# Two accumulators share one output buffer on their way out of a fused attention and softplus-FFN kernel

## The chip, the cores and the metric

The kernel runs on one core of a Trainium2 chip. Its engines work in parallel and are tied by semaphores: TensorE (PE in the profile; its weight loads are listed as PEld), VectorE (DVE), ScalarE (ACT), GpSimd (POOL) and SyncE (SP), which here issues the DMAs. TensorE reads its operands from SBUF and writes to PSUM; results go from PSUM to SBUF by a copy on VectorE or ScalarE, and from SBUF to HBM by a DMA.

The metric is the device time of one execution in microseconds, the median of several runs. All times here are in microseconds (us) unless marked ns.

## What is computed

Eight batches of 576 tokens and 8 heads of width 64. A small set of 32 packed queries per head first attends to all keys and values; then every token attends to the 32 packed results, which serve as its keys and its values. The heads are joined to 512 columns, and a feed-forward layer with softplus follows.

```python
def sm_attn(qq, kk, vv):
    s = scale * np.matmul(qq, kk.transpose(0, 1, 3, 2))
    s = s - np.max(s, axis=-1, keepdims=True)
    a = np.exp(s)
    a = a / (np.sum(a, axis=-1, keepdims=True) + 1e-09)
    return np.matmul(a, vv)
p_packed = sm_attn(p, k, v)
out = sm_attn(q, p_packed, p_packed)
...
h = x @ w_in                     # x: 4608 x 512, w_in: 512 x 2048
g = np.maximum(h, 0.0) + np.log1p(np.exp(-np.abs(h)))
return (g @ w_out).astype(np.float32)      # w_out: 2048 x 512
```

## The kernel before

The hidden layer of 2048 columns is cut into `NF` = 16 blocks of 128. A **unit** is one block of one batch; the main loop (from line 718) runs over the 8 x 16 units in order, batch by batch. Batches are counted from 0.

For each unit, `gemm1` (line 595) makes the 576 hidden values of 128 columns in two halves of 288, in two PSUM buffers named `ph`: twelve matmuls, since each product is taken in three parts (high by high, high by low, low by high) to keep precision. `softplus` turns `ph` into `e`: absolute value, exponential and logarithm on ScalarE (lines 617, 619, 620), maximum and sum on VectorE (line 622), which is the last reader of `ph`. Then `split` (lines 609, 610) cuts the first 512 tokens of `e` into a high part `gh` and a low part `gl` on VectorE. The last 64 tokens go to a collecting tile `rest` on GpSimd (line 626).

Two units later (`LAG` = 2), `gemm2_tile` (line 633) multiplies `gh` and `gl` with the unit's rows of the output weights, three matmuls for each of the `NT` = 4 groups of 128 tokens, and adds them to four PSUM accumulators `acc`. The pool `ps_acc` holds four such buffers and no more. With the sixteenth unit of a batch, the accumulator of a group is complete and `store` (line 648) takes it out: a copy on VectorE (line 650) to an SBUF tile `o`, and from there a DMA or two on SyncE (line 654). Directly behind, the first unit of the next batch begins to add to the same four PSUM buffers, so its first matmul on each waits for that buffer's copy.

Behind an odd batch the 64 remaining tokens of that batch and of the one before it form a fifth group of 128. `rests` (line 657) splits them, 256 columns at a time, into `gh_m` and `gl_m`, runs 48 matmuls into one more buffer of `ps_acc` (`acc_m`), and stores that too. Behind an even batch nothing comes between.

The tiles `o` lie in the pool `cv` under the tag `x`, with two buffers. The same two buffers carry weights in 64-bit form early in the kernel (`load64`, 512 numbers of 8 bytes for each partition), so each is 4 KB long in each partition; an `o` of 512 numbers of 4 bytes fills half of one. The third copy of a batch so takes the buffer of the first, and the fourth that of the second, when the store from it has landed.

In between, the attention of the next batch is worked off in small steps that the main loop draws from a generator (`attention_next` for batches 2 and later). Its names with two numbers, such as `m_4_0`, are those of batch and head group: maximum `m` (line 280), `nm` (282), exponential (287), sum `rs` (292, 293), scores `ps` (267), packed values and the second softmax (lines 334 to 358).

TensorE's order is the one in which the program issues its instructions. The order on the other engines is laid out by a scheduler when the program is built, which follows its own estimate of when each operand and each buffer is there; on the chip each engine then works through its queue in that order.

Of the kernel before, what the change touches and what calls it, by code (L numbers as in the profile page):

```python
# [9 lines left out]
F32 = mybir.dt.float32  # L10
# [16 lines left out]
def pack_attention_then_softplus_ffn(  # L27
# [13 lines left out]
    DM, DFF = w_in.shape  # L41
    P = 128
# [7 lines left out]
    NT = S // P  # L50
    REST = S - NT * P
# [8 lines left out]
    cv = ctx.enter_context(tc.tile_pool(name="cv", bufs=1))  # L60
# [16 lines left out]
    def rest_at(b, f):  # L77

        return f + NF if f < LAG and b // 2 % 2 else f
# [15 lines left out]
    def load_pack(bg, queues):  # L95

        t = cv.tile([PW, H, D], F32, tag="m", name=f"p_{bg}", bufs=1)
        for i in range(BG):
            queues[i % len(queues)].dma_start(
                t[i * J:(i + 1) * J], p[bg * BG + i].rearrange("h j d -> j h d")  # L100
            )
        return t

    def pack_transposed(bg, t):
        for o in range(0, H, HG):
            ps = bank(f"ppt_{bg}_{o}")
            for i in range(HG):
                nc.tensor.transpose(
                    ps[:D, i * PW:(i + 1) * PW], t[:, o + i, :], ident[:PW, :PW]
                )  # L110
            dst = pT[:, o:o + HG, :].rearrange("x h j -> x (h j)")
            nc.vector.tensor_copy(dst[:D], ps[:D, :HG * PW])
            nc.scalar.copy(dst[D:], ps[:D, :HG * PW])
# [414 lines left out]
    def attention(b):  # L528
        return attention_first(b) if b < FIRST else attention_next(b)
# [16 lines left out]
    def m_cols(b):  # L546

        return MC if b else MC // 2
# [30 lines left out]
    def gemm1(b, f, res):  # L579

        n = m_cols(b)
        halves = res["m"][f * P // n]
        at_h, at_l = res["at"]
        phs = []
        for c in range(2):
            ph = ps_h.tile([P, 512], F32, tag="h", name=f"ph_{b}_{f}_{c}")
            phs.append(ph[:, :C])
            i = 0
            for g in range(G):
                mh, ml = halves[g * n // MC]  # L590
                o = g * n % MC + f * P % n
                ms = slice(o, o + P)
                cs = slice(c * C, (c + 1) * C)
                for x, y in ((mh, at_h), (mh, at_l), (ml, at_h)):
                    nc.tensor.matmul(  # L595
                        ph[:, :C], x[:, ms], y[:, g, cs],
                        start=(i == 0), stop=(i == 3 * G - 1),
                    )
                    i += 1
        return phs  # L600

    def halves(nm):
        return [
            work.tile([P, NT * P], F32R, tag=t, name=f"{t}_{nm}", bufs=LAG + 1)
            for t in ("gh", "gl")
        ]

    def split(hi, lo, x):
        nc.vector.tensor_copy(hi, x)  # L609
        nc.vector.tensor_tensor(lo, x, hi.bitcast(F32), op=ALU.subtract)  # L610

    def softplus(b, f, hv, done):
        e = work.tile([P, S], F32, tag="e", name=f"e_{b}_{f}")
        es = [e[:, c * C:(c + 1) * C] for c in range(2)]
        spans = [e] if b == 0 else es
        for c in range(2):
            nc.scalar.activation(es[c], hv[c], AF.Abs)  # L617
            for x in spans[c:c + 1] if b else spans[:c]:
                nc.scalar.activation(x, x, AF.Exp, scale=-1.0)  # L619
                nc.scalar.activation(x, x, AF.Ln, bias=1.0)  # L620
        for c in range(2):
            nc.vector.scalar_tensor_tensor(es[c], hv[c], 0.0, es[c], op0=ALU.max, op1=ALU.add)  # L622
        yield
        yield
        r = (b % 2) * REST
        nc.gpsimd.tensor_copy(rest[:, rest_at(b, f), r:r + REST], e[:, NT * P:])  # L626
        yield
        done[b, f] = halves(f"{b}_{f}")
        split(*done[b, f], e[:, :NT * P])

    def gemm2_tile(acc, gh, gl, f, cs, first, last):
        for i, (x, y) in enumerate(((gh, wo_h), (gh, wo_l), (gl, wo_h))):
            nc.tensor.matmul(  # L633
                acc, x[:, cs], y[:, f, :],
                start=(first and i == 0), stop=(last and i == 2),
            )

    def rows(b, col, n):
        o = out[b * S:(b + 1) * S, :]
        c, t = divmod(col, C)  # L640
        if b < FIRST:
            i, x = divmod(t, NP)
            n = min(n, NP - x)
            return n, o.rearrange("(x s) e -> s x e", s=SI)[2 * i + c, x:x + n, :]
        n = min(n, C - t)
        return n, o.rearrange("(t c) e -> c t e", c=2)[c, t:t + n, :]

    def store(acc, pieces, nm):
        o = cv.tile([P, DM], F32, tag="x", name=f"o_{nm}", bufs=2)
        nc.vector.tensor_copy(o, acc)  # L650
        for row, b, col, n in pieces:
            while n:
                m, dst = rows(b, col, n)
                nc.sync.dma_start(dst, o[row:row + m, :])
                row, col, n = row + m, col + m, n - m

    def rests(b):


        fs = sorted(range(NF), key=lambda x: rest_at(b, x))  # L660
        gh, gl = halves(f"{b}_m")
        n = NT // 2
        for i in range(0, NF, n):
            o = rest_at(b, fs[i])
            c = i % NT * P
            cs = slice(c, c + n * P)
            split(gh[:, cs], gl[:, cs], rest[:, o:o + n, :].rearrange("x f j -> x (f j)"))
            if i == 0:
                yield
                am = ps_acc.tile([P, DM], F32, tag="acc", name=f"acc_{b}_m")  # L670
            for t in range(n):
                gemm2_tile(
                    am, gh, gl, fs[i + t], slice(c + t * P, c + (t + 1) * P),
                    i + t == 0, i + t == NF - 1,
                )
        store(am, [(0, b - 1, NT * P, REST), (REST, b, NT * P, REST)], f"{b}_m")
        yield


# [35 lines left out]
    gs, acc = {}, None  # L715
    units = [(b, f) for b in range(B) for f in range(NF)]
    ahead, chain, due = iter(()), iter(()), 0.0
    for u in range(len(units) + LAG):
        if u < len(units):
            b, f = units[u]  # L720
            if f == 0:
                if (b + 1) % BG == 0 and b + 1 < B:
                    pack_transposed((b + 1) // BG, pt)
                ahead = attention(b + 1) if b + 1 < B else iter(())
                due = 0.0
            chain = softplus(b, f, gemm1(b, f, res[b]), gs)
            next(chain)
            if f == NF - 1:
                if (b + 2) % BG == 0 and b + 2 < B:
                    pt = load_pack((b + 2) // BG, (nc.sync,))  # L730
                for _ in ahead:
                    pass
                if b + 1 < B:
                    weights(b + 1)
        if u >= LAG:
            b2, f2 = units[u - LAG]
            gh, gl = gs.pop((b2, f2))
            if f2 == 0:
                acc = [ps_acc.tile([P, DM], F32, tag="acc", name=f"acc_{b2}_{t}") for t in range(NT)]
        last = u >= LAG and f2 == NF - 1 and b2 % 2 == 1  # L740
        if last:
            both = rests(b2)
            next(both)
        for t in range(NT):
            if u >= LAG:
                gemm2_tile(
                    acc[t], gh, gl, f2, slice(t * P, (t + 1) * P), f2 == 0, f2 == NF - 1
                )
                if f2 == NF - 1:
                    store(acc[t], [(0, b2, t * P, P)], f"{b2}_{t}")  # L750
            if u < len(units):
                due += PACE if b != FIRST - 1 else PACE_FIRST
                while due >= 1:
                    next(ahead, None)
                    due -= 1
                if b == 0:
                    cdue += CONV
                    while cdue >= 1:
                        next(conv, None)
                        cdue -= 1  # L760
            next(chain, None)
        if last:
            next(both)
        if u + 2 < len(units):


            nb, c = units[u + 2][0], units[u + 2][1] * P
            if c % m_cols(nb) == 0:
                make_m(nb, c // m_cols(nb), res[nb])
# [29 lines left out]
```

## Time and profile before

| what | value |
| --- | --- |
| runs, median (lowest to highest) | 786.67 us (784.75 to 788.64) |
| the profiled execution, as a whole | 781.94 us |
| its span in the trace | 780.2 us |
| granted TensorE clock, mean | 0.995 |
| copies of accumulators, line 650 | 32 from `acc`, median 683 ns, first start at 161.7 us, last at 767.0; 4 from `acc_m` of 691 to 692 ns |
| store of an `o`, issue to landing | 1.6 / 2.2 / 4.3 us (least, median, most) |
| share of all DMA engines' time, main queue | 31.4% |

The span is that of the instructions in the trace; the execution has 1.74 us around it. A row of the timeline gives start, duration, engine, line, operation, output and inputs, and in brackets how long the engine sat idle before it and what ended that wait. Buffer numbers are left out of the names, so all four accumulators are `acc` there. The copies of batches 0 to 7 start near 162, 248, 341, 424, 517, 600, 693 and 763 us.

### The profile page before, as it was taken

How to read it: one execution, taken by the hardware profiler on the slowest of the kernel's cores; microseconds unless marked ns; L12 is line 12 of the kernel's file. 1: busy time of each engine (PE TensorE's matmuls, PEld its weight loads, DVE VectorE, ACT ScalarE, POOL GpSimd, SP SyncE). 2: the span in 40 equal slices, each digit the busy share in tenths (PEclk: the TensorE clock that was granted, in tenths of full speed). 3: DMA queues.
4: the chain of work that ended last, by engine and by line, in shares of the span. 5: the costliest groups of instructions: out<-in, count | busy, mean ns of one | idle time of the engine just before them, and what ended most of it. 6: DMA issues, size and time to landing. Idle time of an engine off the chain costs nothing.

```text
span 780.2 us, 14340 instructions
## 1 busy us (share of the span) xinstructions
PE 737.2 (94%) x5360; PEld 580.6 (74%) x5360; DVE 536.8 (69%) x1220; ACT 437.0 (56%) x1089; POOL 93.9 (12%) x166
## 2 busy tenths in 40 slices
PE   6568998889999999999999999999999999999997
PEld 4346675767877787878787787878787787888886
DVE  3788879965778559675877559665887559574553
ACT  6658877655555355566456355565456355565540
POOL 1414433100000000000000000000000000000010
PEclk9999999999999999999999999999999999999999
DMA  9965755424411432025311423025311400010002
GB/s 240 258 159 153 192 137 146 85 60 73 81 32 35 95 54 70 1 70 83 62 31 38 91 47 77 2 56 90 62 32 34 95 2 2 1 55 1 1 1 68
DMA packets 149669, 55.97 MB, mean 72 GB/s; under 512 B 116320, under 2 KB 142944, under 8 KB 149600
## 3 DMA queue, kind: packets, MB, share of 16 engines
q1 hardware_dynamic: 149328, 55.00, 31.4%
q8 instruction: 42, 0.69, 0.4%
q14 instruction: 27, 0.22, 0.1%
q10 hardware_dynamic: 272, 0.07, 0.0%
HBM read 45.61 MB, written 9.44 MB: 71 GB/s over the span
## 4 chain that ended last, share of the span: by engine, by line
PE 81%; DVE 8%; ACT 5%; DMA 3%; issue 2%; POOL 1%; SPq 0%; DVEq 0%; ACTq 0%; POOLq 0%
PE acc L633 40%; PE ph L595 25%; PE acc_m L633 6%; PE psm L558 4%; PE ps L267 2%; PE psp L310 1%; DMA q<-in_q 1%; PE psa L300 1%; DMA x_i<-in_moe_w_in 1%; DVE t L203 1%; ACT e L619 1%; DVE e L622 1%; ACT e L620 1%; ACT m L192 1%; DVE wo_l L236 1%
## 5 line engine op out<-in xcount | busy, mean ns | idle before, releaser
L633 PE MATMUL acc<-wo_h,gh 128*128 128x512 f32 x512 | 208.5, 407 | 5.8 <-DVE o L650 5.8
L622 DVE SCALAR_TENSOR_TENSOR e<-ph,e 128x288 f32<-128x288 f32 x256 | 113.3, 451 | 137.9 <-ACT e L620 135.6
L617 ACT ACTIVATE e<-ph 128x288 f32<-128x288 f32 x256 | 102.7, 402 | 177.9 <-PE ph L595 135.8
L633 PE MATMUL acc<-wo_l,gh 128*128 128x512 f32 x512 | 201.6, 394 | 0.0
L633 PE MATMUL acc<-wo_h,gl 128*128 128x512 f32 x512 | 201.3, 393 | 0.0
L595 PE MATMUL ph<-at_h,mh 128*128 128x288 f32 x512 | 158.7, 310 | 6.9 <-DVE e L622 5.5
L595 PE MATMUL ph<-at_l,mh 128*128 128x288 f32 x512 | 153.0, 299 | 4.3 <-DVE at_l L541 4.3
L595 PE MATMUL ph<-at_h,ml 128*128 128x288 f32 x512 | 153.1, 299 | 0.0
L595 PEld LDWEIGHTS ph<-at_h,mh 128*128 128x128 f32 x512 | 97.4, 190 | 42.9 <-issue 13.9
L633 PEld LDWEIGHTS acc<-wo_h,gh 128*128 128x128 f32 x512 | 96.7, 189 | 32.4 <-DVE o L650 8.2
L626 POOL COPY rest<-e 128x64 f32<-128x64 f32 x128 | 48.3, 378 | 582.8 <-DVE e L622 551.4
L633 PEld LDWEIGHTS acc<-wo_h,gl 128*128 128x128 f32 x512 | 96.6, 189 | 21.5
L619 ACT ACTIVATE e<-e 128x288 f32<-128x288 f32 (+1 forms) x240 | 109.2, 455 | 3.9
L620 ACT ACTIVATE e<-e 128x288 f32<-128x288 f32 (+1 forms) x240 | 109.4, 456 | 3.1
L633 PEld LDWEIGHTS acc<-wo_l,gh 128*128 128x128 f32 x512 | 96.9, 189 | 13.0
L595 PEld LDWEIGHTS ph<-at_l,mh 128*128 128x128 f32 x512 | 97.8, 191 | 7.7 <-DVE at_l L541 5.0
L595 PEld LDWEIGHTS ph<-at_h,ml 128*128 128x128 f32 x512 | 97.8, 191 | 0.0
L610 DVE TENSOR_TENSOR gl<-e,gh 128x512 fp32r<-128x512 f32 x128 | 91.0, 711 | 7.0 <-DVE gh L609 1.4
L573 ACT CAST mh<-psm 128x512 fp32r<-128x512 f32 (+1 forms) x72 | 35.7, 540 | 62.4 <-PE psm L558 62.4
L609 DVE CAST gh<-e 128x512 fp32r<-128x512 f32 x128 | 55.5, 433 | 5.8
L574 DVE TENSOR_TENSOR ml<-psm,mh 128x512 fp32r<-128x512 f32 (+1 forms) x72 | 42.8, 622 | 21.3 <-ACT mh L573 20.7
L558 PE MATMUL psm<-w_in_sb,pt 64*32 64x512 f32 (+1 forms) x576 | 42.3, 567 | 3.4 <-ACT T_q L260 1.2
(75 smaller groups left out, 719.3 us busy)
## 6 DMA issues: line engine op xcount, KB each, us to landing
v<-in_v SPq DMA_DIRECT2D x16, 576.0 KB, 4.8
x_i<-in_moe_w_in SPq DMA_DIRECT2D x32, 256.0 KB, 4.2
x_o<-in_moe_w_out SPq DMA_DIRECT2D x16, 512.0 KB, 4.2
k<-in_k SPq DMA_DIRECT2D x48, 144.0 KB, 3.2
q<-in_q SPq DMA_DIRECT2D x48, 144.0 KB, 3.1
out<-o SPq DMA_DIRECT2D x18, 256.0 KB, 2.2
k<-in_k SPq DMA_DIRECT2D x4, 576.0 KB, 8.6
q<-in_q SPq DMA_DIRECT2D x4, 576.0 KB, 7.3
```

The costliest lines, as they stand in the source:

```text
L558: nc.tensor.matmul(ps[hh * J:(hh + 1) * J, :n], res["pt"][g][o:o + D, hh * J:(hh + 1) * J], w_in_sb[o:o + D, hh, c * n:(c + 1) * n], start ...
L573: nc.scalar.copy(mh[:, cols], ps[:, :n])
L574: nc.vector.tensor_tensor(ml[:, cols], ps[:, :n], mh[:, cols].bitcast(F32), op=ALU.subtract)
L595: nc.tensor.matmul(ph[:, :C], x[:, ms], y[:, g, cs], start=(i == 0), stop=(i == 3 * G - 1),)
L609: nc.vector.tensor_copy(hi, x)
L610: nc.vector.tensor_tensor(lo, x, hi.bitcast(F32), op=ALU.subtract)
L617: nc.scalar.activation(es[c], hv[c], AF.Abs)
L619: nc.scalar.activation(x, x, AF.Exp, scale=-1.0)
L620: nc.scalar.activation(x, x, AF.Ln, bias=1.0)
L622: nc.vector.scalar_tensor_tensor(es[c], hv[c], 0.0, es[c], op0=ALU.max, op1=ALU.add)
L626: nc.gpsimd.tensor_copy(rest[:, rest_at(b, f), r:r + REST], e[:, NT * P:])
L633: nc.tensor.matmul(acc, x[:, cs], y[:, f, :], start=(first and i == 0), stop=(last and i == 2),)
```

## The change

Two accumulators share one tile. For an even group `t` a tile of 128 x 2 x 512 numbers, which fills a whole 4 KB buffer, is taken from the same two buffers; the even group's copy fills its first half and the odd group's its second. So a batch's four copies take two tiles, one per buffer, and the copy of the rests (`t` = 4) takes a third for itself. The stores are the same rows as before, read from a half of the tile.

```diff
-    def store(acc, pieces, nm):
-        o = cv.tile([P, DM], F32, tag="x", name=f"o_{nm}", bufs=2)
+    half = []
+
+    def store(acc, pieces, nm, t):
+        if t % 2 == 0:
+            half[:] = [cv.tile([P, 2, DM], F32, tag="x", name=f"o_{nm}", bufs=2)]
+        o = half[0][:, t % 2, :]
         nc.vector.tensor_copy(o, acc)
...
-        store(am, [(0, b - 1, NT * P, REST), (REST, b, NT * P, REST)], f"{b}_m")
+        store(am, [(0, b - 1, NT * P, REST), (REST, b, NT * P, REST)], f"{b}_m", NT)
...
-                    store(acc[t], [(0, b2, t * P, P)], f"{b2}_{t}")
+                    store(acc[t], [(0, b2, t * P, P)], f"{b2}_{t}", t)
```

The order on TensorE and GpSimd does not change. On VectorE, the copies move, and with them some rows of the attention. In the rows below a name's first number is that of the accumulator or of the unit within its batch, and the last one counts buffers; the change makes `o_0` the tile of accumulators 0 and 1 and `o_2` that of 2 and 3, and line 650 becomes line 654.

VectorE behind batch 0, from the second copy on; before:

```order
L650 COPY o_1_1955<-acc_1_719 128x512
L609 CAST gh_1_1969<-e_1_1934 128x512
L610 TENSOR_TENSOR gl_1_1970<-e_1_1934,gh_1_1969 128x512
L622 SCALAR_TENSOR_TENSOR e_2_1994<-ph_2_0_1980,e_2_1994 128x288
L622 SCALAR_TENSOR_TENSOR e_2_1994<-ph_2_1_1987,e_2_1994 128x288
L650 COPY o_2_1963<-acc_2_720 128x512
L609 CAST gh_2_2019<-e_2_1994 128x512
L610 TENSOR_TENSOR gl_2_2020<-e_2_1994,gh_2_2019 128x512
L650 COPY o_3_1976<-acc_3_721 128x512
```

The same place with the change:

```order
L654 COPY o_0_1946<-acc_1_719 128x512
L654 COPY o_2_1962<-acc_2_720 128x512
L609 CAST gh_1_1968<-e_1_1934 128x512
L654 COPY o_2_1962<-acc_3_721 128x512
L610 TENSOR_TENSOR gl_1_1969<-e_1_1934,gh_1_1968 128x512
L622 SCALAR_TENSOR_TENSOR e_2_1992<-ph_2_0_1978,e_2_1992 128x288
L622 SCALAR_TENSOR_TENSOR e_2_1992<-ph_2_1_1985,e_2_1992 128x288
```

The third and fourth copies now stand around the split of unit 1, ahead of the softplus of unit 2, and no longer among and behind the work of unit 2.

VectorE behind batch 2, in the time of batch 3, from the split of unit 1 on; before:

```order
L609 CAST gh_1_4021<-e_1_3980 128x512
L280 TENSOR_REDUCE m_4_0_4031<-a_4_0_3951 128x1
L610 TENSOR_TENSOR gl_1_4022<-e_1_3980,gh_1_4021 128x512
L650 COPY o_2_4017<-acc_2_3072 128x512
L282 TENSOR_SCALAR nm_4_0_4033<-m_4_0_4031 128x1
L292 TENSOR_SCALAR rs_0_4144<-z_4_0_4072 128x1
L293 RECIPROCAL rs_0_4144<-rs_0_4144 128x1
L622 SCALAR_TENSOR_TENSOR e_2_4051<-ph_2_0_4037,e_2_4051 128x288
L622 SCALAR_TENSOR_TENSOR e_2_4051<-ph_2_1_4044,e_2_4051 128x288
L609 CAST gh_2_4093<-e_2_4051 128x512
L650 COPY o_3_4028<-acc_3_3073 128x512
L610 TENSOR_TENSOR gl_2_4094<-e_2_4051,gh_2_4093 128x512
```

With the change:

```order
L609 CAST gh_1_4016<-e_1_3976 128x512
L654 COPY o_2_4012<-acc_2_3068 128x512
L610 TENSOR_TENSOR gl_1_4017<-e_1_3976,gh_1_4016 128x512
L654 COPY o_2_4012<-acc_3_3069 128x512
L280 TENSOR_REDUCE m_4_0_4025<-a_4_0_3947 128x1
L282 TENSOR_SCALAR nm_4_0_4027<-m_4_0_4025 128x1
L622 SCALAR_TENSOR_TENSOR e_2_4045<-ph_2_0_4031,e_2_4045 128x288
L292 TENSOR_SCALAR rs_0_4138<-z_4_0_4066 128x1
L293 RECIPROCAL rs_0_4138<-rs_0_4138 128x1
L622 SCALAR_TENSOR_TENSOR e_2_4045<-ph_2_1_4038,e_2_4045 128x288
L609 CAST gh_2_4087<-e_2_4045 128x512
L610 TENSOR_TENSOR gl_2_4088<-e_2_4045,gh_2_4087 128x512
```

The fourth copy moves from behind the first half of unit 2's split to directly behind unit 1's, and the softmax maximum of the attention moves behind it. Behind batch 4 the rows are the same.

VectorE behind batch 1, with the splits of the rests, from the second copy on; before:

```order
L650 COPY o_1_2939<-acc_1_2004 128x512
L280 TENSOR_REDUCE m_3_0_2974<-a_3_0_2887 128x1
L609 CAST gh_1_2963<-e_1_2916 128x512
L282 TENSOR_SCALAR nm_3_0_2976<-m_3_0_2974 128x1
L610 TENSOR_TENSOR gl_1_2964<-e_1_2916,gh_1_2963 128x512
L650 COPY o_2_2959<-acc_2_2005 128x512
L609 CAST gh_m<-rest 128x256
L292 TENSOR_SCALAR rs_0_3154<-z_3_0_3082 128x1
L610 TENSOR_TENSOR gl_m<-rest,gh_m 128x256
L293 RECIPROCAL rs_0_3154<-rs_0_3154 128x1
L609 CAST gh_m<-rest 128x256
L650 COPY o_3_2970<-acc_3_2006 128x512
```

With the change:

```order
L654 COPY o_0_2930<-acc_1_2002 128x512
L280 TENSOR_REDUCE m_3_0_2970<-a_3_0_2885 128x1
L654 COPY o_2_2956<-acc_2_2003 128x512
L609 CAST gh_1_2960<-e_1_2914 128x512
L654 COPY o_2_2956<-acc_3_2004 128x512
L610 TENSOR_TENSOR gl_1_2961<-e_1_2914,gh_1_2960 128x512
L282 TENSOR_SCALAR nm_3_0_2972<-m_3_0_2970 128x1
L609 CAST gh_m<-rest 128x256
L610 TENSOR_TENSOR gl_m<-rest,gh_m 128x256
L609 CAST gh_m<-rest 128x256
L610 TENSOR_TENSOR gl_m<-rest,gh_m 128x256
L292 TENSOR_SCALAR rs_0_3150<-z_3_0_3078 128x1
```

The first split of the rests in these rows now has three copies in the rows ahead of it, where it had two, and `nm` stands six places behind the second copy in place of three. Behind batch 4 and batch 2, in the time of batches 3 and 5, rows of the second softmax also change places with rows of units 7 and 8, on VectorE and ScalarE. On SyncE the stores of a batch follow each other more closely, and query loads that stood between them come behind.

## The prediction

> **What bounds the kernel now.** I read the page first, for the busy shares and the costliest groups, then the waits of TensorE, then the timelines of TensorE and VectorE around the places that the waits point to.
>
> ```profile
> span 780.2 us, 14340 instructions
> PE 737.2 (94%) x5360; PEld 580.6 (74%) x5360; DVE 536.8 (69%) x1220; ACT 437.0 (56%) x1089; POOL 93.9 (12%) x166
> L633 PE MATMUL acc<-wo_h,gh 128*128 128x512 f32 x512 | 208.5, 407 | 5.8 <-DVE o L650 5.8
> ```
>
> TensorE (PE) is busy 94% of the span, VectorE (DVE) 69%. The costliest group, the first of the three matmuls that add a unit to an accumulator, has 5.8 us of idle time ahead of it, all ended by the copy in line 650, which is one of the lines that change. When does TensorE wait at all? The first of the changed copies starts at 161.7 us (table ahead of this prediction), and up to it the order of instructions is the same on every engine, so only the time behind it counts. These are all waits of TensorE from 130 us on (microseconds in total, times, longest), and its busy time from 161 us to 780 us:
>
> ```profile
> PE acc L633 <- DVE o L650: 5.8, 4, 1.9
> PE ph L595 <- DVE e L622: 2.0, 1, 2.0
> PE psm L558 <- DVE a L334: 0.6, 1, 0.6
> PE psm L558 <- POOL w_in_sb L211: 0.5, 1, 0.5
> PE ps L267 <- ACT T_q L260: 0.2, 1, 0.2
> 161.00:780.00 619.00, 608.15 (x4360) 486.32 (x4358) 414.27 (x946) 322.89 (x843) 42.51 (x111) 1.00 0.23 47
> ```
>
> In the window TensorE is busy (first figure behind the window's length) 608.15 of 619 us at a granted clock of 1.00; VectorE has 414.27, ScalarE 322.89. The span ends with the copy of the last accumulator and its store:
>
> ```profile
> 775.61 0.69 DVE L650 COPY o_m<-acc_m 128x512 f32<-128x512 f32 x1 [2.12 <-PE acc_m L633]
> ```
>
> So the last matmul sets the end, and time that leaves TensorE's queue there leaves the span, as long as VectorE and ScalarE, which serve it, keep up.
>
> **What the waits cost.** Batches count from 0. Behind an even batch (0, 2, 4, 6) the next batch's first unit needs the four accumulators at once; behind an odd one the rests come between. The first such place lies in the time of batch 1:
>
> ```profile
> 166.26 0.40 PE L633 MATMUL acc<-wo_h,gl 128*128 128x512 f32 x1
> 168.03 0.49 PE L633 MATMUL acc<-wo_h,gh 128*128 128x512 f32 x1 [1.37 <-DVE o L650]
> 168.36 0.39 PE L633 MATMUL acc<-wo_l,gh 128*128 128x512 f32 x1
> 168.59 0.40 PE L633 MATMUL acc<-wo_h,gl 128*128 128x512 f32 x1
> 170.11 0.50 PE L633 MATMUL acc<-wo_h,gh 128*128 128x512 f32 x1 [1.12 <-DVE o L650]
> 170.45 0.40 PE L633 MATMUL acc<-wo_l,gh 128*128 128x512 f32 x1
> ```
>
> Ends of matmuls are modelled and overlap, so I go by starts. Undisturbed, one starts 0.23 us after the other (168.36 to 168.59). Here 166.26 to 168.03 is 1.77, too long by 1.54, and the next step of 0.33 is too long by 0.10. The second wait costs 1.52 - 0.23 = 1.29 and 0.34 - 0.23 = 0.11. Together **3.04 us**. The other three, in the time of batches 3, 5 and 7, with an undisturbed passage from the score matmuls to an accumulator as a measure (its two rows come first):
>
> ```profile
> 248.84 0.72 PE L267 MATMUL ps<-k,pT 64*32 64x288 f32 x16
> 249.48 0.50 PE L633 MATMUL acc<-wo_h,gh 128*128 128x512 f32 x1
> ...
> 347.69 0.72 PE L267 MATMUL ps<-k,pT 64*32 64x288 f32 x16
> 349.89 0.50 PE L633 MATMUL acc<-wo_h,gh 128*128 128x512 f32 x1 [1.48 <-DVE o L650]
> ...
> 523.58 0.71 PE L267 MATMUL ps<-k,pT 64*32 64x288 f32 x16
> 526.16 0.50 PE L633 MATMUL acc<-wo_h,gh 128*128 128x512 f32 x1 [1.87 <-DVE o L650]
> ...
> 697.87 0.39 PE L633 MATMUL acc<-wo_h,gl 128*128 128x512 f32 x1
> 698.22 0.50 PE L633 MATMUL acc<-wo_h,gh 128*128 128x512 f32 x1
> 698.55 0.40 PE L633 MATMUL acc<-wo_l,gh 128*128 128x512 f32 x1
> ```
>
> Undisturbed the passage takes 0.64. In batch 3 it takes 2.20, so **1.56** are lost; in batch 5 2.58, so **1.94**; in batch 7 the steps of 0.35 and 0.33 are too long by 0.12 and 0.10, **0.22**. The four places cost 3.04 + 1.56 + 1.94 + 0.22 = **6.76 us**.
>
> **Why the copies come late.** VectorE works its queue in order. In batch 3:
>
> ```profile
> 344.76 0.68 DVE L650 COPY o<-acc 128x512 f32<-128x512 f32 x1
> ...
> 346.67 0.15 DVE L292 TENSOR_SCALAR rs<-z 128x1 f32<-128x1 f32 x1 [1.17 <-ACT a L287]
> ...
> 348.25 0.46 DVE L622 SCALAR_TENSOR_TENSOR e<-ph,e 128x288 f32<-128x288 f32 x1 [0.72 <-ACT e L620]
> ...
> 349.15 0.68 DVE L650 COPY o<-acc 128x512 f32<-128x512 f32 x1
> ```
>
> The third copy starts at 344.76, the fourth not before 349.15, and TensorE goes on at 349.89. By these rows no accumulator or store holds that copy at 349.15: it stands behind the next unit's work in the queue, which itself waits for ScalarE (1.17 and 0.72). The queue was laid out with the third and fourth copies behind the landing of the first two stores, whose buffers they took. With the change they need no such buffer, and in the order of the changed kernel the third stands directly ahead of the split of the next unit or just behind its first half, and the fourth at most two rows on, behind all eight batches.
>
> **The change, part by part.** The copies and stores stay the same in number and size (36 copies of about 0.68 us); nothing is added or removed on TensorE, whose order is the same row for row. Each second-half copy waits in the order for TensorE alone, not for the store of the first half.
>
> Removed: the 6.76 us. In batch 3 the fourth copy can now start about 344.7 and end at 345.4, three microseconds ahead of its use at 348.33 (347.69 + 0.64); in batch 1 the copies take the places of the splits, so that the third ends about 164.3 and the fourth about 165.3, and TensorE asks at 166.49 and 167.18 (166.26 + 0.23, then three steps). All four waits should go whole.
>
> Moved, behind odd batches: there 48 matmuls on the rests follow the accumulators, fed by splits of 256 columns. The fourth copy now goes ahead of the third split:
>
> ```profile
> 252.13 0.69 DVE L650 COPY o<-acc 128x512 f32<-128x512 f32 x1
> 252.73 0.28 DVE L609 CAST gh_m<-rest 128x256 fp32r<-128x256 f32 x1
> 253.12 0.43 DVE L610 TENSOR_TENSOR gl_m<-rest,gh_m 128x256 fp32r<-128x256 f32 x1
> ...
> 253.69 0.39 PE L633 MATMUL acc_m<-wo_h,gh_m 128*128 128x512 f32 x1
> ...
> 254.15 0.39 PE L633 MATMUL acc_m<-wo_h,gl_m 128*128 128x512 f32 x1
> ```
>
> A copy takes 0.60 of the queue (252.13 to 252.73), so the high part is ready at 253.61 in place of 253.01; the low part, which follows 0.39 behind the start of the high one (252.73 to 253.12), at about 254.15 in place of 253.55. TensorE multiplies with them at 253.69 and 254.15, and loads weights a matmul ahead, 0.23 earlier by the step: at 253.46 and 253.92. The high part is then late by 0.15 and the low one by 0.23. With the signal between the engines I take 0.25 us lost behind each of batches 1, 3 and 5: **0.75**. Behind batch 7 the third split waits for TensorE anyway, and nothing is lost. The ends of this cost are nothing and the whole copy, 3 x 0.60 = 1.8.
>
> What is late next: TensorE reaches the unit behind the relieved wait 1.56 (batch 3) or 1.94 (batch 5) earlier, and its first product needs the buffer that the softplus of the unit before gives up:
>
> ```profile
> 354.73 0.46 DVE L622 SCALAR_TENSOR_TENSOR e<-ph,e 128x288 f32<-128x288 f32 x1 [0.69 <-ACT e L620]
> ...
> 356.60 0.29 PE L595 MATMUL ph<-at_h,mh 128*128 128x288 f32 x1
> ...
> 531.35 0.84 DVE L622 SCALAR_TENSOR_TENSOR e<-ph,e 128x288 f32<-128x288 f32 x2 [1.04 <-ACT e L619]
> 532.85 0.29 PE L595 MATMUL ph<-at_h,mh 128*128 128x288 f32 x1
> ```
>
> If this chain did not move, TensorE would ask at 355.04 for what is free at 355.19, a wait of 0.15, and at 530.91 for what is free about 531.8, 0.9: 1.05 in all. But the chain moves: the fourth copy (0.60) leaves the queue ahead of the softmax maximum on which ScalarE's queue hangs, and part of the chain follows TensorE itself. I take 0 and keep 1.05 for the range. In batches 3 and 5 some softmax rows further on also change places by a row or two; there the margin is small (below), and I take 0.
>
> The stores go out up to 4 us sooner on SyncE's queue, and query loads behind them too. Neither is waited for by TensorE in the waits above, so 0.
>
> Sum: 6.76 - 0.75 = **6.0 us** gained, with 6.8 and 6.76 - 1.8 - 1.05 = 3.9 as its ends. The profiled execution goes from 781.94 to 775.9 (span 774.2). That execution is 4.7 below the median of the runs, so from the median I forecast 786.67 - 6.0 = **780.7 us**.
>
> [...]
>
> **Rivals.**
> *Another wait takes over.* The chains on ScalarE and VectorE, not the copies, end last: the splits behind odd batches cost 1.8, the next unit 1.05, and the unit behind batch 0, where TensorE comes 3.04 earlier, up to as much again as batch 5's 0.9. For it: the splits have no margin left. Against it: the chains get shorter queues ahead of them. The gain is 6.76 - 1.8 - 1.05 - 0.9 = 3.0, so 783.7 us. Chance 0.17.
> *Nothing moves.* The accumulators are the shortage, or the copies are held for a reason that the queue does not show (the second half waiting for the first half's store, which would be the change not doing what it says). For it: four accumulators, all needed at once. Against it: the order names only TensorE for the second halves. 786.7 us. Chance 0.08.
> *Slower.* The reordered softmax rows of batches 3 and 5 hold back a softplus result, and TensorE stands before its next product:
>
> ```profile
> 383.75 0.45 DVE L622 SCALAR_TENSOR_TENSOR e<-ph,e 128x288 f32<-128x288 f32 x1
> ...
> 384.47 0.29 PE L595 MATMUL ph<-at_h,mh 128*128 128x288 f32 x1
> ```
>
> The result is ready at 384.20 and used at 384.47, so it decides from a delay of 0.27 on. The one wait of this kind above, before the stores, cost 2.0. In two units of both batches, that is 8.0 lost against 6.0 gained: 788.7 us. Against it: in the changed order the same activations stand ahead of this result on ScalarE as before, and on VectorE one step of 0.16 more and one transpose less. Chance 0.06.
>
> **How the numbers follow.** The forecast has 0.69. Its own range is a gain of 3.9 to 6.8, 779.9 to 782.8, and the three runs before lie 1.9 below and 2.0 above their median. The range that should hold 8 in 10 goes from 777.0 (full gain and a low median) to 785.5 (takeover and a high median). 0.5% is 3.9 us, about what a measurement of this kernel can tell from no change: faster than 782.7 has nearly the whole forecast and a little of the takeover, 0.70; within it, the rest of takeover and nothing, 0.24; slower 0.06.
>
> **What would show it.** Right: no wait of TensorE for the copy in the store, third and fourth copies within some 4 us of the first in each batch. Behind odd batches: short new waits of the rests' matmuls for their splits. Wrong: gaps before products waiting for softplus in batches 3 and 5, or copies waiting for stores.

## The result, and the profile after

The changed kernel takes 776.14 us (median of 6 runs, 775.54 to 777.86); the kernel before, measured again beside it, 785.04 us (784.33 to 788.64). The ratio is 0.9881 with a 95% interval of 0.9864 to 0.9898, so 8.9 us or 1.2% faster. A second measurement on another chip gave 775.45 against 785.46 us, ratio 0.9868 (0.9846 to 0.9889). The forecast was 6.0 us of gain and a range of 777.0 to 785.5: the direction was right, the gain too small, and the time lies under the range.

The page of the changed kernel's profile: the span, the busy shares, and the group that had 5.8 us of waits.

```profile
span 773.8 us, 14324 instructions
PE 733.0 (95%) x5360; PEld 577.9 (75%) x5360; DVE 539.0 (70%) x1220; ACT 437.0 (56%) x1089; POOL 92.6 (12%) x166
L633 PE MATMUL acc<-wo_h,gh 128*128 128x512 f32 x512 | 207.6, 405 | 0.0
```

The first accumulator matmul no longer waits at all. The only wait of TensorE from 161 us to the end is this one, in the view of its waits:

```profile
PE psm L558 <- DVE a L334: 0.6, 1, 0.6
```

The timelines behind batch 2 (in the time of batch 3), VectorE and then TensorE, answer to the copies that started at 344.76 and 349.15 before, and to the passage of 2.20 us:

```profile
340.73 0.69 DVE L654 COPY o<-acc 128x512 f32<-128x512 f32 x1
...
341.93 0.69 DVE L654 COPY o<-acc 128x512 f32<-128x512 f32 x1
...
344.93 0.72 PE L267 MATMUL ps<-k,pT 64*32 64x288 f32 x16
345.58 0.50 PE L633 MATMUL acc<-wo_h,gh 128*128 128x512 f32 x1
```

The third copy starts 2.26 us behind the first (338.47), the fourth 3.46 behind it, where before they started 3.53 and 7.92 behind it. The passage from the scores to the accumulator takes 0.65.

The starts of each batch's first copy cut the time into stretches that can be compared between traces. Here is the length from one batch's first copy to the next one's; the last column goes from the first copy of batch 6 to the copy of the last rests.

| stretch in the time of batch | 1 | 2 | 3 | 4 | 5 | 6 | 7 and end | sum |
| --- | --- | --- | --- | --- | --- | --- | --- | --- |
| before, first trace | 86.59 | 92.98 | 82.89 | 93.00 | 83.25 | 92.23 | 83.01 | 613.95 |
| changed | 83.48 | 93.04 | 81.34 | 93.03 | 81.33 | 92.26 | 82.75 | 607.23 |
| gained | 3.11 | -0.06 | 1.55 | -0.03 | 1.92 | -0.03 | 0.26 | 6.72 |

So the four relieved places give 6.84 us in this pair of traces, where the prediction had 6.76, and the three ends with rests cost 0.12, where it had 0.75. But the runs gained 8.9, not 6.7. The experiments had to say where the rest comes from.

### The profile page after: what moved, and what is told of

The parts are those of the page before. It is cut to its first block, busy times and chain, and to the rows that moved or that the text cites. A ratio compares the mean times of both kernels' runs of the same rounds, so it can differ in the third digit from the quotient of the medians.

```text
span 773.8 us, 14324 instructions
## 1 busy us (share of the span) xinstructions
PE 733.0 (95%) x5360; PEld 577.9 (75%) x5360; DVE 539.0 (70%) x1220; ACT 437.0 (56%) x1089; POOL 92.6 (12%) x166
## 4 chain that ended last, share of the span: by engine, by line
PE 82%; DVE 8%; ACT 4%; DMA 3%; issue 1%; POOL 1%; SPq 0%; ACTq 0%; DVEq 0%; POOLq 0%
PE acc L633 41%; PE ph L595 26%; PE acc_m L633 6%; PE psm L558 4%; DMA x_o<-in_moe_w_out 2%; PE ps L267 2%; PE psp L310 1%; PE psa L300 1%; ACT m L192 1%; DMA x_i<-in_moe_w_in 1%; DVE t L203 1%; DVE wo_l L236 1%; DVE gl L610 1%; DVE e L622 1%; ACT e L619 1%
```

## The experiments

The theory at this point: the gain is TensorE's waits for copies, which go because there are more free places for the copies. The rivals: that the layout of the paired tile or of its stores matters, that every batch's end gives its part, and that the medians differ from the traces by something that has nothing to do with these waits.

**The kernel before, against itself.** No edit.

> The kernel before, unchanged, against itself. It tells how far two medians of one kernel lie apart and gives a second trace of it. My theory (the gain is the four waits of TensorE for copies and no more, and the profiled execution of before, 781.94 us, was one with a short beginning): ratio 1.000 within 0.002, median 784 to 786 us, and in the trace the waits for the copies are again 5.8 us (6.8 by starts), while the time up to the first copy is some 3 us longer than 161.7. Rival (the profiled execution was a mild case of the waits themselves, since store landings vary): the first copy again near 162 us and waits for the copies of 8 us or more.

The ratio is 1.0007 (0.9992 to 1.0022), median 785.26 us. The trace agrees with neither expectation. Its first copy starts at 161.03, so the beginning was not longer, and the waits for copies are 6.0 us. But the stretch of batch 1 is 89.36 in place of 86.59. TensorE's timeline there:

```profile
167.37 0.49 PE L633 MATMUL acc<-wo_h,gh 128*128 128x512 f32 x1 [1.37 <-DVE o L650]
...
169.46 0.80 PE L633 MATMUL acc<-wo_h,gh 128*128 128x512 f32 x1 [1.12 <-DVE o L650]
170.05 0.63 PE L633 MATMUL acc<-wo_l,gh 128*128 128x512 f32 x1
170.47 0.63 PE L633 MATMUL acc<-wo_h,gl 128*128 128x512 f32 x1
171.03 1.96 PE L558 MATMUL psm<-w_in_sb,pt 64*32 64x512 f32 x16
```

The two waits are those of the first trace to the hundredth. But from 169.46 on a matmul takes 0.63 in place of 0.39, and the sixteen small ones 1.96 in place of 1.09. The view by windows gives the reason. A row of it has the window and its length, then the busy time and number of instructions of PE, PEld, DVE, ACT and POOL, the granted clock (behind the last bracket), and the share and rate of the DMAs. First this trace, then the same place of the first trace of before:

```profile
166.00:169.00 3.00, 0.96 (x3) 0.48 (x3) 2.28 (x5) 0.23 (x1) 0.24 (x1) 0.98 0.20 53
169.00:175.00 6.00, 5.54 (x27) 3.15 (x28) 1.69 (x3) 1.07 (x2) 0.00 (x0) 0.50 0.21 62
```

```profile
167.00:170.00 3.00, 0.96 (x3) 0.48 (x3) 2.54 (x5) 0.00 (x0) 0.24 (x1) 1.00 0.29 79
170.00:176.00 6.00, 5.89 (x54) 3.64 (x55) 2.00 (x5) 3.57 (x10) 0.00 (x0) 1.00 0.17 51
```

In both, TensorE is busy for 0.96 of some 3 us. In one the clock falls to 0.50 behind it, and 27 matmuls run in six microseconds where the other runs 54. The same two waits so cost 2.77 us more in one execution than in the other.

**Halves without free places.** The tile is paired, but the third and fourth accumulators use the same halves again. The order on VectorE is then that of the kernel before.

```diff
-        if t % 2 == 0:
+        if t % NT == 0:
             half[:] = [cv.tile([P, 2, DM], F32, tag="x", name=f"o_{nm}", bufs=2)]
```

> Halves of one tile as in the change, but the third and fourth accumulators go to the same halves as the first two, so each waits for the landing of a store again. My theory (the number of free places counts, not that two share a buffer): the time of before, 784 to 786 us, ratio to before 0.998 to 1.002, waits for the copies 5.8 us again. Rival (the gain comes from how the tile or its stores lie in memory): 776 to 780 us.

784.42 us, ratio 0.9995 (0.998 to 1.0009): the time of before. Its waits:

```profile
PE acc L633 <- DVE o L654: 5.5, 4, 1.9
```

Layout and pairing as such do nothing here; the order of the queue, and with it the gain, changes when four copies have four places (776.14 us).

**Pairs behind even batches alone, and behind odd ones alone.**

```diff
+        if pieces[0][1] % 2 == 0 and t < NT:     # odd ones alone: == 1
+            if t % 2 == 0:
+                half[:] = [cv.tile([P, 2, DM], F32, tag="x", name=f"o_{nm}", bufs=2)]
+            o = half[0][:, t % 2, :]
+        else:
+            o = cv.tile([P, DM], F32, tag="x", name=f"o_{nm}", bufs=2)
```

> Pairs for the batches 0, 2, 4 and 6 alone; the odd batches store as before. My theory (only behind even batches does TensorE wait for copies): the whole gain, within 0.3 us of the changed kernel, 776 to 777 us, and no new delay of 0.1 us in all behind batches 1, 3 and 5. Rival (each of the eight places gives its part, by the queues of VectorE and SyncE): about half, 780 to 781 us.

> Pairs for the batches 1, 3, 5 and 7 alone. My theory: nothing, 784 to 786 us (0.1 us slower in the trace, less than the runs can tell), with waits for the copies of 5.8 us as before. Rival (each of the eight places gives its part): about half of the gain, 780 to 781 us.

Even ones alone: 775.97 us, ratio 0.9885 (0.9863 to 0.9907), the whole gain. The stretches of batches 2, 4 and 6 are 93.00, 92.99 and 92.22, so the 0.12 of the ends with rests is gone; the runs can't tell so little. Odd ones alone: 785.39 us, ratio 1.001 (0.9997 to 1.0023), nothing. Both as the theory has it, but for the waits of the latter, 6.5 us in all where 5.8 were expected: its third copy of batch 5 waited 1.44 us for a store to land, and the fourth came later with it. TensorE's wait there was the longest of its kind yet, and the clock held (line 657 is the copy in this kernel):

```profile
529.15 0.50 PE L633 MATMUL acc<-wo_h,gh 128*128 128x512 f32 x1 [2.55 <-DVE o L657]
...
528.00:530.00 2.00, 0.84 (x3) 0.48 (x3) 1.92 (x4) 0.07 (x1) 0.49 (x1) 1.00 0.09 18
530.00:532.00 2.00, 2.00 (x24) 1.12 (x24) 0.83 (x4) 1.35 (x4) 0.00 (x0) 1.00 1.03 225
```

**Filling the waits.** If idle time of TensorE costs clock, the kernel before must get faster when its waits are filled with matmuls that nothing reads, though the copies come no sooner. This kernel computes what the other does, with 19 matmuls more; the order on all other engines is that of before.

```diff
+    FILL = {(1, 2): 6, (1, 3): 5, (3, 3): 4, (5, 3): 4}
...
         for t in range(NT):
+            if u >= LAG and f2 == 0 and (b2, t) in FILL:
+                fill = ps_m.tile([P, 512], F32, tag="m", name=f"fill_{b2}_{t}")
+                for i in range(FILL[b2, t]):
+                    nc.tensor.matmul(fill, wo_h[:, 0, :P], wo_h[:, 1, :], start=True, stop=True)
```

> The kernel before with matmuls that nothing reads put into TensorE's waits: 6 and 5 ahead of the third and fourth accumulator in batch 1, 4 ahead of the fourth in batches 3 and 5, each 0.23 us and so shorter than the wait. The copies come as late as before. Clock theory (the second traces of before show the granted clock at 0.50 for some 5 us behind the two waits in batch 1, and the profiled execution of before did not; idle time of TensorE costs more than its length in most executions): a clock of 1.00 in that place, and a median some 2.5 us under that of before, 782 to 783.3 us. Rival (what the runs gain beyond the 6.7 us of the trace has nothing to do with idle time): the time of before, 784.5 to 786 us, or some tenths more.

> The kernel before with filled waits again. Clock theory: 2.2 to 5.4 us under the kernel before (2.2 is 8.9 less 6.7, 5.4 the first measurement), and again a granted clock of 1.00 behind all four places. Rival: within 1 us of the kernel before.

First 781.26 us against 786.61, ratio 0.993 (0.9909 to 0.9951); again, on the chip of the second measurement, 782.49 against 785.46, ratio 0.996 (0.9945 to 0.9974). So more work in the queue makes the kernel 2.0 to 4.3 us faster by the second interval. The second time lies where it was expected. The first lies below its 782 to 783.3: its gain of 5.4 us is twice what was forecast, and why isn't known, except that the median of before on that chip stands 1.2 to 1.6 us above those of the other chips. TensorE's timeline and the windows of the second:

```profile
170.58 1.52 PE L749 MATMUL fill<-wo_h 128*128 128x512 f32 x6
172.12 0.50 PE L633 MATMUL acc<-wo_h,gh 128*128 128x512 f32 x1
...
172.92 1.31 PE L749 MATMUL fill<-wo_h 128*128 128x512 f32 x5
174.20 0.50 PE L633 MATMUL acc<-wo_h,gh 128*128 128x512 f32 x1
...
165.00:171.00 6.00, 6.00 (x33) 5.21 (x32) 3.60 (x8) 3.85 (x11) 0.24 (x1) 1.00 0.34 87
171.00:177.00 6.00, 5.98 (x38) 3.54 (x37) 2.84 (x6) 0.77 (x2) 0.24 (x1) 1.00 0.31 89
```

The accumulators still start late, 6.36 and 8.44 us behind the first copy (165.76) where the first trace of before had 6.37 and 8.45; batch 1's stretch is 86.57, as in that trace. But TensorE is busy all through, and the clock stays at 1.00, there and behind the other places, in both traces (in batches 3 and 5 a wait of 0.49 is left ahead of the fill). The medians are near the first trace of before, 781.94 us, where the clock had stayed at 1.00 behind the same waits without a fill. The two filled executions that were profiled took 779.97 and 785.70 us; their stretches are the same, and the difference lies ahead of the first copy, which starts at 160.08 and 165.76, in a part that the edit doesn't touch. One thing more is different: in both filled traces the third copy of batch 5 doesn't wait for a store, and that stretch is 82.89, under the 83.25 of the first trace. Why, two traces don't tell.

**The changed kernel again, and two more traces of before.** No edits. These ran on the chip of the second filled kernel.

> The changed kernel again, on one chip with the next three. Clock theory (gain = the waits, 6.7 us by the traces, plus what the clock loses behind them, a matter of chance in each execution): 6.3 to 7.0 us under the kernel with filled waits, and a spread of the runs of some 2 us against 4 or more before. Rival (waits alone make the gain, and medians of different chips do not compare): filled waits gain nothing beyond 1 us, and the changed kernel is 8 to 9 us under both.

> The kernel before once more, for its trace alone. Clock theory: waits of 5.5 to 6.6 us as in all traces, and where the granted clock falls to 0.50 behind one of them, the stretch from the first copies of that batch to the next batch's is 1 to 3 us longer than 86.6 (batch 1), 82.9 (batch 3) or 82.9 to 84 (batch 5) us; it falls in at least one place in most traces. Rival: the clock stays at 1.00 and the time is above 784 us all the same.

> The same as ctl2, a further trace, with the same expectations.

The changed kernel, 775.45 us, is 7.0 us under the filled one (expected: 6.3 to 7.0). Its six runs spread over 2.9 us, seventeen of before over 5.4; twelve of the filled kernel spread over 4.6, so the spread says little. Its trace has the stretches of the first one to 0.01 each. The two traces of before, one run each (786.90 and 785.85 us), have the clock at 0.50 behind batch 0 and behind batch 4. In the last, the copy, the accumulator and the clock in batch 5:

```profile
523.60 0.69 DVE L650 COPY o<-acc 128x512 f32<-128x512 f32 x1 [1.41 <-DMA out<-o]
...
528.51 0.79 PE L633 MATMUL acc<-wo_h,gh 128*128 128x512 f32 x1 [2.55 <-DVE o L650]
...
528.50:531.50 3.00, 2.99 (x19) 1.06 (x19) 1.69 (x5) 0.87 (x2) 0.00 (x0) 0.50 0.76 163
```

Two things went wrong here that the first trace showed small or not at all: the store of the first accumulator landed later, so that the third copy waited 1.41 us for its buffer in place of 0.53, and the clock fell. The stretch is 85.70, 4.37 above that of the changed kernel, where the first trace had 1.92.

**One place by itself.** Pairs behind batch 0 alone, and behind batches 2, 4 and 6 alone: the edit above with `pieces[0][1] == 0` and with `in (2, 4, 6)`.

> Pairs behind batch 0 alone. Clock theory: the 3.1 us of the two waits there and most of the loss by the clock, which was seen there in two of four traces with these waits: 779.2 to 780.5 us. Rival (the whole 8.9 us are waits, spread as in the first trace, 3.04 of 6.76): 785.1 - 4.0 = 781.1 us.

> Pairs behind batches 2, 4 and 6 alone. Clock theory: the 3.7 us of the waits there and little more: 781 to 781.8 us, and the slow clock in batch 1 stays in part of the executions. Rival (8.9 us of waits in the proportion of the first trace): 785.1 - 4.9 = 780.2 us.

780.24 us, ratio 0.9917 (0.9897 to 0.9937), and 780.76 us, ratio 0.9918 (0.9895 to 0.994), against a median of 786.61 on that chip. The first agrees with the clock theory, the second lies between the two expectations. The gains, 6.4 and 5.9 us by the medians, add up to more than the 8.9 and 10.0 of the whole change, against a median of before that was 1.2 to 1.6 us above those of the other chips. How the gain is shared out between the places isn't settled by these runs. The second one's trace has the clock drop behind batch 0 once more (stretch of 88.11).

**One half for all four.** Each copy waits for the landing of the store before it.

```diff
-        o = half[0][:, t % 2, :]
+        o = half[0][:, 0, :]        # and a new tile at t % NT == 0 alone
```

> All four accumulators of a batch go out through one half of one tile, so each copy waits for the landing of the store before it. By landings of 2.2 us the fourth copy comes some 4 to 5 us later than before, at four places: waits of TensorE for copies of 20 us or more in place of 5.8. Clock theory: the granted clock falls to 0.50 behind the waits at three or four of the four places, and the time rises by several microseconds more than the waits, to 803 to 812 us. Rival (the clock does not hang on the waits): the clock stays at 1.00 behind most of them, 797 to 802 us.

816.22 us in the one run that there is, above both expectations. Its waits for copies, and the windows of batch 1:

```profile
PE acc L633 <- DVE o L654: 24.8, 9, 4.2
...
172.00:178.00 6.00, 2.57 (x5) 1.66 (x6) 1.39 (x2) 0.00 (x0) 0.00 (x0) 0.52 0.18 52
178.00:184.00 6.00, 6.00 (x41) 3.28 (x48) 1.29 (x2) 2.33 (x6) 0.00 (x0) 0.63 0.13 39
```

In batch 1 TensorE waits 2.07, 3.17 and 1.86, 7.1 us in all, and the stretch is 94.52, 11.0 above that of the changed kernel. Much of the other 3.9 goes with the half clock that shows in both windows. The clock fell behind the other three places too: its mean is 0.57 from 359 to 371 us, 0.53 from 544 to 555 and 0.57 from 728 to 736.

## Why the prediction missed

**What held.** TensorE's waits for copies are where the gain comes from; they go whole, with no wait in their place, as the order rows had let expect. In the pair of profiled executions the four places give 6.84 us where 6.76 were summed, place by place 3.11, 1.55, 1.92 and 0.26 for 3.04, 1.56, 1.94 and 0.22, and the span is 773.8 where 774.2 was forecast. The next unit's product doesn't wait (the 1.05 kept for the range), the reordered softmax rows of batches 3 and 5 cost nothing, and no second half waits for the store of the first.

**The splits of the rests, a term too large.** The prediction had 0.75 us behind batches 1, 3 and 5; it is 0.12. The timelines of VectorE, TensorE and its weight loads behind batch 1:

```profile
250.31 0.15 DVE L282 TENSOR_SCALAR nm<-m 128x1 f32<-128x1 f32 x1
250.37 0.29 DVE L609 CAST gh_m<-rest 128x256 fp32r<-128x256 f32 x1
250.76 0.43 DVE L610 TENSOR_TENSOR gl_m<-rest,gh_m 128x256 fp32r<-128x256 f32 x1
...
250.87 0.40 PE L633 MATMUL acc_m<-wo_h,gh_m 128*128 128x512 f32 x1
...
251.34 0.41 PE L633 MATMUL acc_m<-wo_h,gl_m 128*128 128x512 f32 x1
251.24 0.19 PEld L633 LDWEIGHTS acc_m<-wo_h,gl_m 128*128 128x128 f32 x1 [0.17 <-DVE gl_m L610]
```

Two steps were off. Counted from the first matmul of the rests (248.15; before 250.97), the two parts are ready 0.47 and 0.46 later than before, not 0.60, because `nm` now holds the queue for 0.06 (250.31 to 250.37) in place of 0.19 (251.33 to 251.52 before). So the high part, ready at 250.66, is in time for 250.87. The low part is ready at 251.19, its weights load 0.05 later, and the matmul starts 0.10 behind that: here the weights had no full matmul of lead, which the prediction asked for, and the matmul came late by some hundredths only. The whole delay is some 0.04 a place.

**The price of a wait, the step that failed.** "What the waits cost" priced each wait by its own length, 6.76 us, from one execution in which the granted clock was 1.00 from 161 us on. Seven traces have the waits in batch 1, and seven those in batch 5:

| trace | batch 1 | batch 5 | clock at 0.50 behind the waits |
| --- | --- | --- | --- |
| before, first | 86.59 | 83.25 | nowhere |
| before against itself | 89.36 | 83.44 | batch 1 |
| before, last two | 88.11, 88.11 | 85.32, 85.70 | 1 and 5, in both |
| halves without free places | 87.63 | 84.82 | 1 and 5 |
| pairs behind odd batches | 86.56 | 84.20 | nowhere; batch 5 waited 2.55 |
| pairs behind 2, 4 and 6 | 88.11 | relieved | batch 1 |
| pairs behind 0 | relieved | 83.32 | nowhere |

The clock fell behind five of seven pairs of waits in batch 1 and behind three of seven single ones in batch 5, and never behind the 1.48 us of batch 3. The mean of batch 1 is 87.78, 1.19 above the first trace, that of batch 5 84.29, 1.04 above it. With these 2.2 us the waits cost 6.72 + 2.2 = 8.9 us in a mean execution, which is what the runs gained. The agreement is better than so few traces can promise; the second measurement has 10.0. Whole traces say the same: from the first copy of batch 0 to that of the last rests the four traces of the kernel before take 613.95, 616.87, 617.53 and 617.90 us, the two of the changed one 607.23 and 607.22, 9.3 apart in the mean. Most of the 2.2 is the clock; a part in batch 5 is the later landing of a store, up to 1.44 us of wait for the third copy where the first trace had 0.53 (0.36 more in the mean of the seven). So the first trace was a mild case on both counts: its execution of 781.94 us lies under all six of the measurement beside the change and near the fastest of the 29 of a later one (781.79). The prediction saw that it lay 4.7 under the median and took the same 6.0 off both, as if the difference were scatter that the change would not touch.

The filled kernel, 3.0 and 5.4 us faster by the medians with the clock at 1.00, shows that this loss hangs on TensorE's idle time here. It doesn't part the clock from the landing in batch 5, since both were absent from its traces; in batch 1, where no copy of these traces waited for a store, only the clock is left.

Behind which waits did the clock fall? Their length alone doesn't tell: it held behind one of 2.55 us and fell behind one of 1.90. The traces show more. Within a trace the half clock set in and ended on one grid of 3.413 us: in the last trace of before it lasts from 170.12 to 173.53 and from 528.52 to 531.93, 358.40 us or 105 steps apart. The grid didn't keep step with the program: the same waits are cut differently from trace to trace. These are steps around the two waits in batch 1 (before against itself, two in a row, then the first trace of before) and around a wait of 2.55 in batch 5 (the last trace of before, then the pairs behind odd batches):

```profile
165.44:168.85 3.41, 1.52 (x6) 0.60 (x4) 2.59 (x6) 0.76 (x2) 0.24 (x1) 1.00 0.15 38
168.85:172.27 3.42, 2.81 (x19) 1.06 (x19) 0.55 (x1) 0.00 (x0) 0.00 (x0) 0.50 0.41 122
...
167.72:171.14 3.42, 1.99 (x14) 1.11 (x22) 1.88 (x4) 0.00 (x0) 0.00 (x0) 1.00 0.35 99
...
525.11:528.52 3.41, 0.86 (x18) 0.19 (x17) 2.33 (x7) 2.25 (x8) 0.49 (x1) 1.00 0.56 120
...
524.68:528.09 3.41, 1.93 (x21) 0.67 (x19) 1.57 (x7) 2.97 (x8) 0.00 (x0) 1.00 0.54 118
```

TensorE is busy for 0.45 of the first step and 0.25 of the fourth, and at the end of both the clock falls. It is busy for 0.58 of the third and 0.57 of the last, and the clock holds. Around the waits of batches 1, 3 and 5 in the seven traces that have those of batch 1, the clock fell behind each of the five steps that were busy for 0.45 or less (0.45, 0.44, 0.32, 0.30 and 0.25), behind three of four between 0.46 and 0.50 (0.47, 0.49 and 0.50; it held behind 0.46, in batch 5 of the first trace), and behind none of 0.57 or more (there are none between). The step with the single wait of batch 3 was never under 0.57 in them. At half clock, the second row with 0.82 didn't bring the full clock back; it came back behind the next step, 172.27 to 175.68, busy throughout. This was read from the traces afterwards; no run was made to test it, and the shares rest on modelled ends of matmuls.

**The base and the range.** The point lay 4.6 us too high: 2.9 by the gain, 1.6 by the median of before, which came out at 785.04 in six runs where three had given 786.67. Of the 2.9, some 0.7 are the splits (0.63) and the hundredths at the four places, and 2.2 the price of the waits. The range's low end took the full 6.8 us and a low median as the best case; by the figures given that is 784.75 - 6.8 = 778.0, so 777.0 stands one lower than its terms. It had no term for a wait that costs more than its length, and the time came 0.9 us under it. The takeover and the slower case, with 0.23 of the chances, did not show in any row.

## What to carry to other kernels

Where a buffer's slot is larger than what lies in it, let two tenants share it before looking for memory: what kept the copies early in VectorE's queue here was the number of places that are free without waiting for a store (776.14 us with four, 784.42 with two in the same tile), and the order of the built program shows before any run whether the copies move. An idle gap of the engine that sets the time can cost more than its length (here 8.9 us went with 6.72 of waits): look at the granted clock behind it, at the idle time that falls within one step of its grid (3.413 us here), and at more than one execution, above all when the profiled execution is faster than the runs (781.94 us here, where their median was 785.04). If gaps can't be removed, matmuls that nothing reads may be worth putting into them (3.0 and 5.4 us here).

## What was not expected of the hardware

The granted TensorE clock fell to 0.50 behind two waits of 1.37 and 1.12 us close together (0.77 for the second in one trace), in five traces of seven, and cost the stretch 1.0 to 2.8 us; behind single waits of 1.87 to 2.55 us it fell in three traces of seven. It fell at the edge of a grid of 3.413 us, behind steps of which TensorE was busy for half or less. Nineteen matmuls of 0.23 us that nothing reads, 4.4 us of work put into those waits, made the kernel 3 us faster (ratio 0.996, 0.9945 to 0.9974; on another chip 0.993, 0.9909 to 0.9951).
